# Weight conversion two steps ahead in the first block, an unconditional first single tile, and expert weights requested in halves

## The chip, the cores and the metric

The kernel runs on one core of one Trainium2 chip. Its engines work side by side, each through its own queue in program order: TensorE (PE, matmuls; PEld is its weight load), VectorE (DVE), ScalarE (ACT), GpSimd (POOL) and SyncE (SP, which only issues DMAs here). They wait for each other through semaphores. The metric is the device time of one execution in microseconds.

## The reference

Attention with pooled keys and values, then a dense feed-forward layer, then a layer of routed experts; each stage's output is the next one's input.

```python
k_p = k.reshape(B, H, Sp, pool, D).mean(axis=3)        # B=8, H=8, S=576, D=64, pool=8
v_p = v.reshape(B, H, Sp, pool, D).mean(axis=3)
scores = scale * np.matmul(q, k_p.transpose(0, 1, 3, 2))
attn = softmax(scores)                                 # over 72 pooled keys
x = (attn @ v_p)  -> [4608, 512]
...
h = x @ w_in                                           # w_in float64 [512, 2048]
g = np.where(h >= 1, h, np.where(h <= -1, 0.0, (h + 1) ** 2 / 4.0))
x = g @ w_out                                          # w_out float64 [2048, 512]
...
expert_idx = np.argmax(x @ w_gate, axis=1)             # 8 experts
for e in range(E):                                     # w1[e] [512, 1024], w2[e] [1024, 512]
    h = np.maximum(xe @ w1[e], 0.0)
    out[mask] = gate_w[mask, None] * (h @ w2[e])
```

w_in and w_out arrive as float64. With the inputs that reference.py draws, experts 0, 4, 6 and 7 get 3905, 577, 14 and 112 tokens and the others none, that is 31, 5, 1 and 1 tiles of 128 tokens.

## The kernel before

**Join of attention and feed-forward.** The 36 token tiles are cut into ten blocks (`BLK`: 3, then seven of 4, then 3 and 2). Three tiles (`HEAD`) go through attention first, by a hand-written order (`line`). Then the loop over `steps` runs block j and hidden slice m of 16: `f1(j, m + 2)` computes a slice of 128 hidden units two steps ahead (`AHEAD`), `slot(j, 2m)` does side work, `f2(j, m)` multiplies slice m by its piece of w_out, and `slot(j, 2m + 1)` does side work again. Side work is attention of the next block's tiles (`run_units`: `u_qt` transposes q, `u_sc_all` makes scores and their exponential, `u_turn_p`, `u_place_p` and `u_pv` the rest), pooling of k and v (`kv`), and, in block 0 only, `tick`.

**tick.** In block 0 the float64 weights are fetched and turned into two float32 parts, high and low, held in W (first layer) and WO (second layer). A tick takes three pieces of w_in or w_out at three stages: ACT converts (`convert_a`, lines 522 and 526), DVE merges bits (`convert_b`, lines 534 and 537, handed out by `mix`), ACT writes the high part (`convert_c`, line 544) and POOL the low part (`low_part`, line 264); SP stores the WO piece to DRAM for the later blocks and requests a raw piece five ticks ahead. The list `order` sets which piece each tick takes. `FG` holds f1's results: lines 595 (DVE), 596 (ACT), 600 (DVE), 601 (ACT) and 264 (DVE). `later` and `flush` hand work of one slot to the next flush.

**Experts.** The expert with most tokens goes first, in groups of 4 tiles (lines 977 to 994); the tiles that are left are "single tiles" (`last_slot`). With the counts above these are seven: five of expert 4, one of 6, one of 7. Before a single tile of a new expert, ACT and DVE turn the staged float32 weights (ST1, ST2) into high and low parts (`cvt1_half`, lines 1060 and 1061; `cvt2`, lines 1052 and 1053), inside a branch on a table entry (`if_changed`). SP requests the next expert's w1 into ST1 and w2 into ST2 (`fetch_next`, line 1086) by DMAs that run or not by another table entry: in the kernel before, at the first tile of an expert. A skipped one appears in the trace as an issue of about 0.07 us. Per single tile PE runs `u_h` (1023 to 1025) into two banks, ACT writes them to EH (1026), PE transposes EH (1031), and `u_y2` (1042 to 1044) gives the output. DMA completions are counted on eight queue lanes taken in turn; after branches of different length join, the write of EH's second half waits for the lane count that the taken branch reaches with its last request.

Of the kernel before, what the change touches and what calls it, by code (L numbers as in the profile page):

```python
# [13 lines left out]
ACTF = mybir.ActivationFunctionType  # L14
# [10 lines left out]
def attention_ffn_routed_experts_kernel(  # L25
# [278 lines left out]
    def u_sc_all(t):  # L304
        pbs = [bank(), bank()]
        for c in range(4):
            for g in range(2):
                toks = slice(64 * g, 64 * g + 64)
                kb = KB[(t * 128 + 64 * g) // S % 2]
                for i in range(2):  # L310
                    rows = slice(64 * i, 64 * i + 64)
                    nc.tensor.matmul(pbs[i][toks, c * SP_:(c + 1) * SP_],  # L312
                                     qt_of(t)[rows, c * 128 + 64 * g:c * 128 + 64 * g + 64],
                                     kb[rows, c], start=True, stop=True)
        sc, sc3, smx = sc_of(t), sc3_of(t), smx3[:, t % 3]
        for i in range(2):
            src = pbs[i][:, 0:4 * SP_].rearrange("p (h c) -> p h c", h=4)
            hs = slice(i, H, 2)
            nc.vector.tensor_reduce(out=smx[:, hs], in_=src, axis=AX.X, op=ALU.max)
            mix()  # L320
            nc.vector.tensor_tensor(out=sc3[:, hs], in0=src,
                                    in1=smx[:, hs].to_broadcast([128, 4, SP_]), op=ALU.subtract)
        nc.scalar.activation(out=sc, in_=sc, func=ACTF.Exp, scale=1.0 / 64)
        wide[0] = True
        finish(t)

    smx3 = sb.tile([128, 3, H, 1], F32, name="smx3")
    ssm3 = sb.tile([128, 3, H, 1], F32, name="ssm3")
# [174 lines left out]
    def load_raw(m, o, i):  # L503
        if o:
            src = w_out[m * 128:(m + 1) * 128, :].bitcast(I32).rearrange("p (a x) -> p a x", a=8)
            nc.sync.dma_start(out=RB[i], in_=src)
        else:
            src = w_in[:, m * 128:(m + 1) * 128].bitcast(I32)
            src = src.rearrange("(c p) (a x) -> p c a x", p=128, a=2)
            for c in range(KD):  # L510
                nc.sync.dma_start(out=RB[i][:, 2 * c:2 * c + 2], in_=src[:, c])

    def cvt_dst(i):
        m, o = order[i]
# [33 lines left out]


    FIRST, MORE = AHEAD + 2, 1  # L550
    order = [(m, 0) for m in range(FIRST)] + [(0, 1)]
    PER = []
    n = FIRST
    for m in range(1, KF):
        more = min(MORE, KF - n)
        order += [(m, 1)] + [(n + i, 0) for i in range(more)]
        PER.append(1 + more)
        n += more
    PER.append(0)
    CAHEAD = order.index((1, 1)) - 1  # L560
    ticks = [0]

    def more_raw(i):
# [307 lines left out]
    def table_2():  # L871

        V = Steps()
        st, en, t1, t2 = tv["st"], tv["en"], tv["t1"], tv["t2"]
        V.tensor_reduce(out=tv["tot"], in_=tv["nte"], axis=AX.X, op=ALU.add)
        V.tensor_tensor(out=tv["tot"], in0=tv["tot"], in1=tv["beg"], op=ALU.subtract)
        V.tensor_copy(TB[:, 3:4], tv["tot"])

        def following(end, nx, hn):

            V.tensor_scalar(t1, st, end, None, op0=ALU.is_equal)
            V.tensor_tensor(out=t1, in0=t1, in1=tv["nte"], op=ALU.mult)
            V.tensor_scalar(t1, t1, 0.0, None, op0=ALU.is_gt)
            V.tensor_reduce(out=tv["hn"], in_=t1, axis=AX.X, op=ALU.add)
            sel(V, "nx", "io")
            V.tensor_copy(nx, tv["nx"])
            if hn is not None:
                V.tensor_copy(hn, tv["hn"])

        following(tv["ntf"], TB[:, 6:7], TB[:, 7:8])  # L890
        V.tensor_tensor(out=t1, in0=tv["ind"], in1=en, op=ALU.mult)
        V.tensor_reduce(out=tv["enj"], in_=t1, axis=AX.X, op=ALU.add)
        following(tv["enj"], TB[:, 2:3], None)
        V.tensor_tensor(out=t1, in0=tv["ind"], in1=tv["io"], op=ALU.mult)
        V.tensor_reduce(out=tv["ej"], in_=t1, axis=AX.X, op=ALU.add)
        V.tensor_scalar(tv["jp"], tv["js"], -1.0, None, op0=ALU.add)
        V.tensor_scalar(t1, st, tv["jp"], None, op0=ALU.is_le)
        V.tensor_scalar(t2, en, tv["jp"], None, op0=ALU.is_gt)
        V.tensor_tensor(out=t1, in0=t1, in1=t2, op=ALU.mult)
        sel(V, "ep", "io")  # L900
        V.tensor_tensor(out=tv["ch"], in0=tv["ej"], in1=tv["ep"], op=ALU.not_equal)
        V.tensor_tensor(out=tv["jp"], in0=pcol, in1=tv["tot"], op=ALU.is_lt)
        V.tensor_tensor(out=tv["ch"], in0=tv["ch"], in1=tv["jp"], op=ALU.mult)
        V.tensor_copy(TB[:, 0:1], tv["ch"])
        V.tensor_tensor(out=tv["ch"], in0=tv["ch"], in1=tv["hn"], op=ALU.mult)
        V.tensor_copy(TB[:, 1:2], tv["ch"])
        return V.ops
# [161 lines left out]
        for i in range(2):  # L1069
            cvt2(hf, i)  # L1070

    def if_changed(j, f, engines):
        r = nc.values_load(TB[j:j + 1, 0:1], engines=engines, min_val=0, max_val=1)
        with tc.If(r > 0):
            f()

    def fetch_next(j, which, hf=None, col=(1, 2)):

        cv = nc.values_load(TB[j:j + 1, col[0]:col[0] + 1], engines=[SP], min_val=0, max_val=1)
        ev = nc.values_load(TB[j:j + 1, col[1]:col[1] + 1], engines=[SP], min_val=0, max_val=NE - 1)  # L1080
        src, dst = ((w1, ST1), (w2, ST2))[which]
        src = src[bass.ds(ev, 1)].rearrange("o (c p) f -> p (o c) f", p=128)
        if hf is not None:
            cs = slice(4 * hf, 4 * hf + 4)
            src, dst = src[:, cs], dst[:, cs]
        nc.sync.dma_start(out=dst, in_=src, cond=cv > 0, cond_hint=False)


    with tc.manual_schedule():
# [6 lines left out]
        def head_pool(i, eng):  # L1096
            pool_kv(0, i, raw0[i], eng)
# [26 lines left out]
        hu[1][0]()  # L1124
        for c in range(2, 4):
            u_kt_pair(0, c)
        hu[0][2]()
        for i in (8, 10, 12):
            head_pool(i, nc.gpsimd)
        hu[1][2]()  # L1130
        head_pool(9, nc.vector)
        tick()
        hu[2][0]()
        flush()
        head_pool(14, nc.gpsimd)
        head_pool(11, nc.vector)
        hu[2][2]()
        head_pool(13, nc.vector)
        head_pool(15, nc.vector)
        load_pair(0)  # L1140
        load_pair(1)
        tick()
        flush()
        kv = deque([pair_step(c) for c in range(4)] + [kv_step(1, i) for i in range(H, 2 * H)])
        line = [(0, 3), (0, 5), (1, 3), (0, 6), (1, 5), (2, 3), (1, 6), (2, 5), (2, 6)]
        for i, (t, n) in enumerate(line):
            hu[t][n]()
            flush()
            if i in (1, 4, 6):
                tick()  # L1150
        while ticks[0] < CAHEAD + 3:
            tick()
        banks.clear()
        banks.extend(ps[6:8])
# [16 lines left out]
        def slot(j, s):  # L1171

            want = min(state["units"], -(-(s + 1) * state["units"] // (22 if j == NB - 2 else 29 - 2 * AHEAD + 2)))
            wide[0] = False
            run_units(want - state["done"])
            state["done"] = max(want, state["done"])
            flush()
            if j == 0:
                for _ in range(min(1, PER[s // 2]) if s % 2 == 0 else PER[s // 2] - 1):
                    tick()  # L1180
                if kv:
                    kv.popleft()()
            for _ in range(2 if j >= NB - 2 else 0 if wide[0] else 1 + s % 2):
                if todo:
                    todo.popleft()()
# [27 lines left out]
        for m in range(AHEAD):  # L1213
            f1(0, m)
            flush()
        for g, (j, m) in enumerate(steps):
            if m == 0:
                if j:
# [76 lines left out]
        nq = nc.values_load(TB[0:1, 5:6], min_val=0, max_val=NQ)  # L1295

        def first_weights():
            if_changed(0, cvt1_all, [ACT, DVE])
            fetch_next(0, 0)

        def step_a(qn):
            for m in range(AHEAD):
# [66 lines left out]
        def last_slot(j):  # L1369
            if j + DEEP + 1 < MAXR:  # L1370
                fetch_last(j + DEEP + 1)
            if_changed(j, lambda: cvt2_half(0), [ACT, DVE])
            fetch_next(j, 1, 0)
            if j and j + DEEP < MAXR:
                r_gather(j + DEEP)
            u_h(j, 0)
            u_h(j, 1)
            u_th(j % 2, 0, bank())
            if j + 1 < MAXR:
                if_changed(j + 1, lambda: cvt1_half(0), [ACT, DVE])  # L1380
            if j:
                y_end(j - 1)
            if j and j + DEEP - 1 < MAXR:
                r_tx(j + DEEP - 1)
            u_th(j % 2, 1, bank())
            if j + 1 < MAXR:
                if_changed(j + 1, lambda: cvt1_half(1), [ACT, DVE])
                fetch_next(j + 1, 0)
            if_changed(j, lambda: cvt2_half(1), [ACT, DVE])
            fetch_next(j, 1, 1)  # L1390
            u_y2(j % 2, 0, ps[4 + j % 2])

# [45 lines left out]
```

## Time and profile before

| | |
|---|---|
| time, median of 3 runs | 1418.43 us (1416.07 to 1423.02) |
| the profiled execution's own time | 1422.48 us |
| its span (first to last instruction) | 1420.5 us |
| PE busy | 1363.9 us, 96% of the span |
| DVE, ACT, POOL busy | 769.4, 434.3, 360.0 us |
| mean granted TensorE clock | 0.98 of full speed |

PE is busy almost throughout, so 56.6 us of the span are without a matmul, and the share of the clock below full speed is in the first 160 us and near the end. A row of waits names the waiting engine and line, what released it, the total in us, how often, and the longest. A row of a timeline gives start, duration, engine, line, operation, output and input, count, and in brackets the idle time just before and its releaser.

### The profile page before, as it was taken

The numbers are of one execution on the slowest core, as the hardware profiler recorded it, in microseconds if no ns is written. First come the engines' busy times: TensorE is split into PE (matmuls) and PEld (weight loads), VectorE is DVE, ScalarE is ACT, GpSimd is POOL, SyncE is SP. The second block draws the span as 40 slices with busy tenths as digits, with TensorE's granted clock in tenths as the row PEclk, the third lists the DMA queues.
The fourth block names the chain that finished last, engine by engine and source line by source line (L and its number), as shares of the span: only waits on it lengthen the run. The fifth ranks groups of instructions, "written<-read, shape, count | busy, mean of one in ns | idle before, by whom it ended". The sixth has DMA issues, their size and how long they took to land.

```text
span 1420.5 us, 22119 instructions
## 1 busy us (share of the span) xinstructions
PE 1363.9 (96%) x8082; PEld 1119.8 (79%) x8082; DVE 769.4 (54%) x1573; ACT 434.3 (31%) x729; POOL 360.0 (25%) x517
## 2 busy tenths in 40 slices
PE   5888999999999999999999999999999999999897
PEld 4766778878878878788788788889878888888685
DVE  5677557566666666675666556456433223333335
ACT  4566432222232223223222233342111111112234
POOL 4284644203304202413310011031231121110211
PEclk9889999999999999999999999999999999999999
DMA  8687557446546445644553344572543322332504
GB/s 223 214 264 239 178 145 208 131 136 184 155 133 181 158 134 178 169 158 142 164 155 109 109 138 157 191 248 75 186 127 104 104 87 76 112 104 74 172 31 156
DMA packets 170414, 213.47 MB, mean 150 GB/s; under 512 B 84167, under 2 KB 115175, under 8 KB 170280
## 3 DMA queue, kind: packets, MB, share of 16 engines
q1 hardware_dynamic: 135704, 102.30, 24.8%
q10 hardware_dynamic: 26784, 88.16, 18.6%
q0 software_dynamic: 7792, 21.35, 4.7%
q8 instruction: 69, 1.13, 0.3%
q14 instruction: 65, 0.53, 0.1%
HBM read 188.30 MB, written 47.03 MB: 166 GB/s over the span
## 4 chain that ended last, share of the span: by engine, by line
PE 80%; issue 6%; DVE 4%; DMA 4%; ACT 2%; POOL 1%; SPq 1%; POOLq 0%; ACTq 0%; another core or an unknown queue 0%; DVEq 0%
PE ps L588 9%; PE ps L616 9%; PE ps L590 9%; PE ps L589 9%; PE ps L617 8%; PE ps L618 8%; PE ps L978 4%; PE ps L979 4%; PE ps L977 4%; PE ps L992 3%; PE ps L993 3%; PE ps L994 3%; PE ps L419 3%; PE ps L312 1%; DMA Y<-in_moe_w_out_dram 1%
## 5 line engine op out<-in xcount | busy, mean ns | idle before, releaser
L588 PE MATMUL ps<-XT,W 128*128 128x512 f32 (+2 forms) x640 | 243.7, 381 | 3.5 <-DVE FG L264 2.0
L590 PE MATMUL ps<-XT,W 128*128 128x512 f32 (+2 forms) x640 | 237.9, 372 | 4.6 <-POOL W L264 4.6
L616 PE MATMUL ps<-WO,FG 128*128 128x512 f32 x576 | 233.3, 405 | 5.0 <-ACT WO L544 4.9
L589 PE MATMUL ps<-XT,W 128*128 128x512 f32 (+2 forms) x640 | 238.0, 372 | 0.0
L617 PE MATMUL ps<-WO,FG 128*128 128x512 f32 x576 | 228.5, 397 | 6.5 <-POOL WO L264 6.5
L618 PE MATMUL ps<-WO,FG 128*128 128x512 f32 x576 | 227.3, 395 | 0.0
L596 ACT ACTIVATE FX<-FX,half 128x512 f32<-128x512 f32 (+2 forms) x152 | 104.0, 684 | 388.3 <-DVE FX L595 356.3
L595 DVE TENSOR_SCALAR FX<-ps 128x512 f32<-128x512 f32 (+2 forms) x152 | 96.8, 637 | 120.1 <-PE ps L590 118.2
L588 PEld LDWEIGHTS ps<-XT,W 128*128 128x128 f32 x640 | 122.2, 191 | 27.2 <-DVE FG L264 2.8
L714 POOL DMA_INDIRECT perm_d<-idt,POSI x36 | 35.3, 981 | 416.2 <-DVE SM L700 352.9
L590 PEld LDWEIGHTS ps<-XT,W 128*128 128x128 f32 x640 | 121.7, 190 | 23.4 <-POOL W L264 5.2
L983 DVE SCALAR_TENSOR_TENSOR FG<-ps,FG 128x512 fp32r<-128x512 f32 (+1 forms) x64 | 43.2, 675 | 177.7 <-ACT FG L982 175.2
L600 DVE TENSOR_TENSOR ps<-FX,ps 128x512 f32<-128x512 f32 (+2 forms) x152 | 97.6, 642 | 75.7 <-ACT FX L596 75.7
L589 PEld LDWEIGHTS ps<-XT,W 128*128 128x128 f32 x640 | 122.1, 191 | 17.6
L616 PEld LDWEIGHTS ps<-WO,FG 128*128 128x128 f32 x576 | 109.5, 190 | 31.0 <-ACT WO L544 5.6
L617 PEld LDWEIGHTS ps<-WO,FG 128*128 128x128 f32 x576 | 109.9, 191 | 27.9 <-POOL WO L264 7.8
L618 PEld LDWEIGHTS ps<-WO,FG 128*128 128x128 f32 x576 | 109.9, 191 | 23.8
L601 ACT ACTIVATE FG<-ps 128x512 fp32r<-128x512 f32 (+2 forms) x160 | 88.9, 555 | 120.2 <-DVE ps L600 105.7
L264 DVE TENSOR_TENSOR FG<-ps,FG 128x512 fp32r<-128x512 f32 (+2 forms) x160 | 100.7, 629 | 43.4 <-ACT FG L601 41.3
L252 POOL TENSOR_TENSOR AT<-AT 72x256 f32<-72x256 f32 x106 | 81.1, 765 | 135.2 <-DMA AT<-in_v_dram 67.5
L982 ACT ACTIVATE FG<-ps 128x512 fp32r<-128x512 f32 (+1 forms) x64 | 37.4, 585 | 246.3 <-PE ps L979 232.7
L977 PE MATMUL ps<-XT,W 128*128 128x512 f32 (+1 forms) x256 | 98.9, 386 | 1.4 <-ACT XT L961 1.4
(228 smaller groups left out, 2174.2 us busy)
## 6 DMA issues: line engine op xcount, KB each, us to landing
WO<-wo_d ACTq DMA_DIRECT2D x144, 512.0 KB
AT<-in_moe_w_dram SPq DMA_DIRECT2D x10, 2048.0 KB
AT<-in_moe_w_dram SPq DMA_DIRECT2D x14, 1024.0 KB
p_d<-AT SPq DMA_DIRECT2D x29, 384.0 KB
AT<-in_v_dram SPq DMA_DIRECT2D x59, 144.0 KB
wo_d<-WO SPq DMA_DIRECT2D x16, 512.0 KB
AT<-in_k_dram SPq DMA_DIRECT2D x56, 144.0 KB
PT<-p_d SPq DMA_DIRECT2D x58, 128.0 KB
```

The lines of the kernel that those rows point to most:

```text
L264: eng.tensor_tensor(out=lo, in0=x, in1=r32(hi), op=ALU.subtract)
L588: nc.tensor.matmul(o, wi(m, 0, c), xh, start=(c == 0), stop=False)
L589: nc.tensor.matmul(o, wi(m, 0, c), xl, start=False, stop=False)
L590: nc.tensor.matmul(o, wi(m, 1, c), xh, start=False, stop=(c == KD - 1))
L595: nc.vector.tensor_scalar(r, o, -1.0, 1.0, op0=ALU.max, op1=ALU.min)
L596: nc.scalar.activation(out=r, in_=r, func=ACTF.Square, scale=0.5, bias=half)
L600: nc.vector.tensor_tensor(out=o, in0=r, in1=o, op=ALU.max)
L601: nc.scalar.activation(out=gh, in_=o, func=ACTF.Copy)
L616: nc.tensor.matmul(o, gh, WO[:, g % 4, 0], start=(m == 0), stop=False)
L617: nc.tensor.matmul(o, gh, WO[:, g % 4, 1], start=False, stop=False)
L618: nc.tensor.matmul(o, gl, WO[:, g % 4, 0], start=False, stop=(m == KF - 1))
L977: nc.tensor.matmul(o, e1(0)[:, c, ms], xh, start=(c == 0), stop=False)
```

## The change

- `order` gets (1, 1) right behind (0, 1), so that every piece of w_out from the second on is taken one step earlier than before; `PER` and `CAHEAD` follow. The number of pieces is the same.
- In `slot(0, s)` the tick stands ahead of the units and of flush, not behind them. Two of the early ticks stand behind f1(0, 0) and f1(0, 1).
- In `u_sc_all` of tiles 3 to 8 the exponential is handed to `later`, so it stands behind the flush's other work.
- In the head, the q transpose of tile 2 comes ahead of the first tick, and one v pooling goes from DVE to POOL.
- A raw piece of w_in is requested by one DMA in place of four.
- The first single tile converts its weights without a branch, and the next expert's weights are requested at the last tile of an expert, not at the first; w1 is requested in two halves by columns.

```diff
@@ u_sc_all
-        nc.scalar.activation(out=sc, in_=sc, func=ACTF.Exp, scale=1.0 / 64)
         wide[0] = True
-        finish(t)
+
+        def exps():
+            nc.scalar.activation(out=sc, in_=sc, func=ACTF.Exp, scale=1.0 / 64)
+            finish(t)
+        if HEAD <= t < TURN0:
+            later.append(exps)
+        else:
+            exps()
@@ load_raw
-            src = src.rearrange("(c p) (a x) -> p c a x", p=128, a=2)
-            for c in range(KD):
-                nc.sync.dma_start(out=RB[i][:, 2 * c:2 * c + 2], in_=src[:, c])
+            nc.sync.dma_start(out=RB[i].rearrange("p (c a) x -> p c (a x)", a=2),
+                              in_=src.rearrange("(c p) x -> p c x", p=128))
@@
-    order = [(m, 0) for m in range(FIRST)] + [(0, 1)]
+    order = [(m, 0) for m in range(FIRST)] + [(0, 1), (1, 1)]
...
-    for m in range(1, KF):
+    for m in range(2, KF):
...
-    PER.append(0)
-    CAHEAD = order.index((1, 1)) - 1
+    PER += [0, 0]
+    CAHEAD = order.index((2, 1)) - 1
@@ table_2
-        following(tv["ntf"], TB[:, 6:7], TB[:, 7:8])
+        following(tv["ntf"], TB[:, 6:7])
+        V.tensor_tensor(out=tv["ch"], in0=tv["ntf"], in1=tv["beg"], op=ALU.is_equal)
+        V.tensor_tensor(out=tv["ch"], in0=tv["ch"], in1=tv["hn"], op=ALU.mult)
+        V.tensor_copy(TB[:, 7:8], tv["ch"])
...
+        V.tensor_scalar(tv["ep"], tv["js"], 1.0, None, op0=ALU.add)
+        V.tensor_tensor(out=tv["ch"], in0=tv["enj"], in1=tv["ep"], op=ALU.is_equal)
+        V.tensor_tensor(out=tv["ch"], in0=tv["ch"], in1=tv["jp"], op=ALU.mult)
         V.tensor_tensor(out=tv["ch"], in0=tv["ch"], in1=tv["hn"], op=ALU.mult)
         V.tensor_copy(TB[:, 1:2], tv["ch"])
@@ fetch_next
-        if hf is not None:
+        if hf is not None and which:
             cs = slice(4 * hf, 4 * hf + 4)
             src, dst = src[:, cs], dst[:, cs]
+        elif hf is not None:
+            fs = slice(hf * 512, (hf + 1) * 512)
+            src, dst = src[:, :, fs], dst[:, :, fs]
@@ the head
-        while ticks[0] < CAHEAD + 3:
+        while ticks[0] < CAHEAD + 1:
             tick()
@@ slot
             wide[0] = False
+            if j == 0:
+                for _ in range(min(1, PER[s // 2]) if s % 2 == 0 else PER[s // 2] - 1):
+                    tick()
             run_units(want - state["done"])
             state["done"] = max(want, state["done"])
             flush()
-            if j == 0:
-                for _ in range(min(1, PER[s // 2]) if s % 2 == 0 else PER[s // 2] - 1):
-                    tick()
-                if kv:
-                    kv.popleft()()
+            if j == 0 and kv:
+                kv.popleft()()
@@ the loop's start
         for m in range(AHEAD):
             f1(0, m)
             flush()
+            tick()
@@ first_weights, last_slot
-            if_changed(0, cvt1_all, [ACT, DVE])
-            fetch_next(0, 0)
+            cvt1_all()
+            for hf in range(2):
+                fetch_next(0, 0, hf)
...
-                if_changed(j + 1, lambda: cvt1_half(0), [ACT, DVE])
+                of_tile(j + 1, lambda: cvt1_half(0))
+                fetch_next(j + 1, 0, 0)
...
-                if_changed(j + 1, lambda: cvt1_half(1), [ACT, DVE])
-                fetch_next(j + 1, 0)
+                of_tile(j + 1, lambda: cvt1_half(1))
+                fetch_next(j + 1, 0, 1)
```

What this moves on the engines, at three places. The first is ACT in block 0, where the scores of tile 5 are made; before (L323 is the exponential, L601 f1's result FG, L544 the high part of WO or W):

```order
L596 ACTIVATE AT<-AT,half 128x384
L323 ACTIVATE AT<-AT 128x576
L601 ACTIVATE FG<-ps_73 128x384
L544 ACTIVATE WO<-FX 128x512
L522 ACTIVATE FX<-WG 128x512
L526 ACTIVATE WG<-WG 128x512
L544 ACTIVATE W<-FX 128x512
```

The same place of the change (lines are shifted: L326 is the exponential, L606 FG, L549 the high part):

```order
L601 ACTIVATE AT<-AT,half 128x384
L549 ACTIVATE WO<-FX 128x512
L527 ACTIVATE FX<-Y 128x512
L531 ACTIVATE WG<-Y 128x512
L606 ACTIVATE FG<-ps_73 128x384
L326 ACTIVATE AT<-AT 128x576
L549 ACTIVATE W<-FX 128x512
```

The WO piece went from behind the exponential to ahead of FG, and it is a piece for one step later; the W piece still stands behind the exponential.

The second place is ACT in the head, before (L323 the exponentials of tiles 0 and 1, L522 and L526 the first tick, L362 the copy of tile 2's transposed q, then the exponential of tile 2):

```order
L323 ACTIVATE AT<-AT 128x576 x2
L522 ACTIVATE FX<-Y 128x512
L526 ACTIVATE WG<-Y 128x512
L362 ACTIVATE AT<-ps_75 128x512
L323 ACTIVATE AT<-AT 128x576
```

And in the change:

```order
L326 ACTIVATE AT<-AT 128x576 x2
L368 ACTIVATE AT<-ps_75 128x512
L326 ACTIVATE AT<-AT 128x576
L527 ACTIVATE FX<-Y 128x512
L531 ACTIVATE WG<-Y 128x512
```

The copy of q and the exponential of tile 2 went ahead of the first tick.

The third place is ACT at the first single tile, before (L1060 and L1052 convert w1 and w2, L1026 writes EH; L1073 and L1074 load a table entry and branch on it):

```order
L1074 COMPARE_AND_BRANCH
L1060 ACTIVATE W<-AT 128x2x512 x4
L1074 UNCONDITIONAL_BRANCH x2
L1355 UNCONDITIONAL_BRANCH
L1393 TENSOR_LOAD TB
L1073 TENSOR_LOAD TB
L1073 ISA x2
L1074 COMPARE_AND_BRANCH
L1052 ACTIVATE W<-AT 128x1024 x2
L1074 UNCONDITIONAL_BRANCH x2
L1026 ACTIVATE FX<-ps_72 128x512
L1026 ACTIVATE FX<-ps_73 128x512
```

And in the change (L1070, L1062, L1036 are the same three operations):

```order
L1070 ACTIVATE W<-AT 128x2x512 x4
L1373 UNCONDITIONAL_BRANCH
L1412 TENSOR_LOAD TB
L1062 ACTIVATE W<-AT 128x1024 x2
L1036 ACTIVATE FX<-ps_72 128x512
L1036 ACTIVATE FX<-ps_73 128x512
```

The two branches of the first single tile are gone; the conversions and the writes of EH follow each other in the same order.

## Rows read from the trace of the kernel before

**Rows 1.** The page: granted clock in 40 slices of 35.5 us, in tenths.

```profile
PEclk9889999999999999999999999999999999999999
```

**Rows 2.** Waits of PE in the first 250 us: total, times, longest.

```profile
PE ps L617 <- POOL WO L264: 6.5, 3, 2.8
PE ps L312 <- ACT AT L362: 6.2, 1, 6.2
...
PE ps L616 <- ACT WO L544: 4.9, 3, 2.0
PE ps L590 <- POOL W L264: 4.6, 2, 2.6
...
PE ps L588 <- DVE FG L264: 1.7, 1, 1.7
```

**Rows 3.** Busy time of each engine in block 0 from its second step on.

```profile
core 0: us, PE busy (x) PEld busy (x) DVE busy (x) ACT busy (x) POOL busy (x), PEclk, DMA share, GB/s
57.80:155.84 98.04, 81.76 (x568) 68.42 (x566) 73.30 (x132) 64.46 (x116) 61.02 (x68) 0.85 0.71 229
```

**Rows 4.** The timeline around one of block 0's stalls.

```profile
94.66 0.68 ACT L323 ACTIVATE AT<-AT 128x576 f32<-128x576 f32 x1 [3.22 <-DVE AT L321]
...
95.62 0.62 ACT L544 ACTIVATE WO<-FX 128x512 fp32r<-128x512 f32 x1
...
96.29 0.50 PE L616 MATMUL ps<-WO,FG 128*128 128x512 f32 x1 [1.38 <-ACT WO L544]
...
97.82 1.72 POOL L264 TENSOR_TENSOR WO<-FX,WO 128x512 fp32r<-128x512 f32 x1
...
99.60 0.79 PE L617 MATMUL ps<-WO,FG 128*128 128x512 f32 x1 [2.81 <-POOL WO L264]
```

**Rows 5.** Windows of 1 us around that stall; columns as in group 3.

```profile
97.00:98.00 1.00, 0.00 (x0) 0.00 (x0) 0.51 (x1) 1.00 (x3) 1.00 (x2) 0.77 0.96 298
...
104.00:105.00 1.00, 1.00 (x7) 1.00 (x6) 0.81 (x2) 0.85 (x2) 0.92 (x3) 0.82 0.85 211
```

**Rows 6.** DVE groups by line and form, 57 to 156 us: count, busy, mean ns.

```profile
L537 DVE SCALAR_TENSOR_TENSOR FX<-FX,ps 128x512 int32<-128x512 int32 x25 | 17.1, 683 | 0.9
...
L534 DVE SCALAR_TENSOR_TENSOR ps<-Y,WG 128x512 int32<-128x512 int32 x9 | 8.9, 984 | 0.9 <-ACT WG L526 0.9
```

**Rows 7.** The timeline of the head, at ACT's first tick and at f1's start.

```profile
20.86 0.67 ACT L522 ACTIVATE FX<-Y 128x512 f32<-128x512 f32 x1 [2.10 <-DMA Y<-in_moe_w_in_dram]
...
22.68 1.24 PE L312 MATMUL ps<-AT 64*64 64x72 f32 x32 [6.21 <-ACT AT L362]
...
26.35 0.68 ACT L323 ACTIVATE AT<-AT 128x576 f32<-128x576 f32 x1 [3.72 <-DVE AT L321]
...
39.78 0.69 PE L588 MATMUL ps<-XT,W 128*128 128x384 f32 x1 [1.42 <-DVE XT L426]
```

**Rows 8.** The chain that ended last, at the first single tile.

```profile
1316.13 10.60 DMA AT<-in_moe_w_dram
1326.99 0.61 ACT FX L1026
```

**Rows 9.** Windows of the first single tile; columns as in group 3.

```profile
1321.50:1328.40 6.90, 1.38 (x9) 1.12 (x8) 0.57 (x2) 1.09 (x2) 0.99 (x2) 0.85 0.62 215
1328.40:1333.40 5.00, 5.00 (x14) 3.97 (x13) 2.58 (x4) 2.60 (x3) 1.19 (x1) 0.52 0.49 189
```

**Rows 10.** Waits of PE from 1000 us on.

```profile
PE ps L1031 <- ACT FX L1026: 5.5, 1, 5.5
PE ps L1024 <- DVE W L1061: 1.8, 2, 1.2
...
PE ps L1042 <- ACT W L1052: 1.2, 1, 1.2
```

**Rows 11.** SP and ACT timeline where the last expert's w1 is requested and used.

```profile
1384.88 2.28 SPq L1086 DMA_DIRECT2D AT<-in_moe_w_dram  x2
...
1393.54 2.01 ACT L1060 ACTIVATE W<-AT 128x1024 fp32r<-128x1024 f32 x2 [4.19 <-DMA AT<-in_moe_w_dram]
```

## The prediction on record

> **What bounds the kernel now.** I read the clock first [rows 1]: TensorE is granted full speed nearly everywhere, and what is missing lies in the first four slices, in the head and block 0. Outside them PE is busy, so a gain can come only from places where PE waits or runs slow. The list of PE's waits names those in block 0 [rows 2]: the second-layer weights, 4.9 us for their high part (ACT) and 6.5 us for their low part (POOL), and the first-layer weights, 4.6 us for the low part; in the head, 6.2 us for the copy of tile 2's q. The window over block 0 from its second step on [rows 3] gives the size: 98.04 us, PE busy for 81.76, so 16.28 us of waits, of which the three weight rows are 16.0. The mean granted clock there is 0.85. [...]
>
> The timeline shows how one of those stalls comes about [rows 4]. ACT's exponential of the scores waits 3.22 us for DVE, and the high part of WO stands behind it at 95.62; PE's line 616 waits for that, the low part follows at 97.82 to 99.54 on POOL, and line 617 waits 2.81 us more. TensorE is still at full clock when it stops, falls to the low level during the stall, and is back only near 104.2 [rows 5]. A late conversion is paid twice: in the wait and in the slow stretch behind it.
>
> Near the end, the chain that ended last goes through a 10.60 us transfer from 1316.13 to ACT's second write of EH at 1326.99 [rows 8]. The transfer is the request for expert 6's w1, which no one needs for four more tiles; the write waits for the queue lane that it sits on. PE waits 5.5 us there [rows 10].
>
> **Term 1, block 0.** Each WO piece is now taken a whole step earlier and ahead of the slot's units, and the exponential stands behind it. In the stall of [rows 4] PE needed the piece 1.38 us before its high part and 4.4 us before its low part was there; a step is 98.04 / 14 = 7.0 us with stalls and about 5 without, so it comes in time. The WO rows are 11.4 of 16.0 us of waits [rows 2], 71%. With the same share of the slow clock (8.7 us) they are worth 20.1 us. The exponential does not vanish: the W piece still stands behind it. In the example W's high part would follow the exponential's end (95.3) by 0.6 us and its low part by 1.3 to 1.7 more, so it is ready at about 97.5, and PE, not held up by WO, would need it at about 97.3 (nine matmuls of the second layer at 0.23 us each and a unit behind 94.3). I take 1 us off for it: 19 us.
>
> Bounds: the ceiling is the next engine. DVE is busy for 73.30 us of the window [rows 3], so the gain can't pass 98.04 - 73.30 = 24.7 us. The floor is that W's waits grow as WO's go: I set 5 us.
>
> [...] On DVE, line 537 reads one operand from PSUM and takes 683 ns; line 534, which reads both from SBUF, takes 984 ns on average in one form [rows 6], while POOL is busy 62% of the window [rows 3]. [...]
>
> **Term 2, the head.** ACT was idle 2.10 us before 20.86 for raw weights that its first tick needs, and tile 2's q was copied only behind that tick; PE waited until 22.68 [rows 7]. The copy is now ahead of the tick, so it can start at 20.86 - 2.10 = 18.76, take 0.6 and let PE start at about 19.4: 3.3 us earlier. One tick more (1.2 us of ACT) then stands behind tile 2's exponential, so about 2.1 reach f1's start, now 39.78 [rows 7]. The first f2 needs only the first WO piece, which has the time of two f1 calls. DVE is relieved of one pooling, POOL takes it while it waits for sums. I take 2.5 us; bounds 0 and the whole wait, 6.2.
>
> **Term 3, the first single tile.** Expert 4 has five tiles, so at its first tile the request is now skipped, and nothing large sits on the lane. Of the 6.90 - 1.38 = 5.52 us without a matmul [rows 9] about 0.5 stay, because the second transposes still need ACT's 0.6 us write. The next 5.00 us had a mean clock of 0.52 with PE busy throughout: 2.4 us lost, of which I take 2. Together 7.0 us. The two branches gone save ACT and DVE time that PE doesn't wait for once the request is away: nothing. Bounds 0 (a skipped request that holds its lane) and 7.9.
>
> **Term 4, the last tiles.** Requests move from an expert's first tile to its last. Expert 6 is asked for at tile 4 and not at tile 0, so both of the last changes of expert happen as one did before: w1 asked for at 1384.88, used at 1393.54 after ACT had waited 4.19 us [rows 11], PE waiting 1.8 us for w1 and 1.2 for w2 [rows 10]. Asking in halves lets the first half go as soon as its half of the stage is converted, about 4 us earlier. I take the two as equal: 0. Bounds: 3.0 us won, or 3.0 lost at the change to expert 6.
>
> **Edits at nothing.** One request for a w_in piece in place of four saves SP's issue time. PE's waits name the conversions, not raw data [rows 2]; without that cover a late piece would show as ACT waiting for a DMA, at 2.1 us each as in the head. The few added small DVE operations that fill the table lie beside matmuls, under the last dense block, where PE's clock and work are full [rows 1].
>
> **Sum.** 19 + 2.5 + 7 + 0 = 28.5 us. Against the profiled execution (1422.48 us; span 1420.5 and 2 around it) that gives 1394.0; that execution was 4.05 above the median of the runs, 1418.43, from which it gives 1389.9. I predict **1390 us**.
>
> **Rivals.**
> - A, the forecast: waits for WO go, W's stay small. 1377 to 1400. For it: the cause in [rows 4] is a place in a queue, and the place changes. Chance 0.58.
> - B, block 0 becomes bound by DVE and by W behind the exponential, and gives 5 to 14 us, not 19. For it: DVE's 73.30 us and [rows 6]; the W rows of [rows 2] exist already. Against it: 25% of DVE's time is free. With 8 us the time is 1418.4 - 8 - 2.5 - 6 = 1402. Chance 0.25.
> - C, the stalls only change their name: each WO wait becomes a W or DMA wait of the same length, with its slow stretch, and only the first single tile's 7 us come: 1411.4, at the edge of what can be told from no change. For it: DMA share 0.71 in the window [rows 3]. Against it: no row of [rows 2] waits for raw weights. Chance 0.10.
> - D, slower. The tick's three ACT operations (0.62 [rows 4], 0.67 [rows 7] and the like, 1.9 us) now stand between f1's square and the copy to FG, and so before PE gets f1's bank back. [...] Against it: PE waited for FG once before, 1.7 us [rows 2], and the bank is needed only two f1 later. Chance 0.05.
>
> What is left, 0.02, is none of these. A measurement of this kernel can tell about 0.5%, 7 us, from no change. A and B are faster by more than that (0.83), C and part of the rest the same (0.12), D slower (0.05). The range must reach over B: from the ceilings of the terms (24.7 + 6.2 + 7.9 + 3.0 = 41.8, 1377) to B's slow end, 1376 to 1410; A's own is 1377 to 1400.
>
> **What would show it.** Right: in the changed profile PE's waits for WO in block 0 are below 2 us, the block from its second step on takes about 79 us with a mean clock over 0.95, f1 starts near 37.5, the first single tile has less than 1 us between its transposes, and one more short wait for w1 or w2 stands two tiles before the end. B would show as PE waits for W or FG with DVE over 85% busy in the block; C as equal idle time under another name; D as a wait at nearly every f1. The prediction is wrong if PE's waits in block 0 stay above 10 us, if the second write of EH still waits for a DMA, or if the two last changes of expert cost more than 6 us.

## The result and the profile after

| | before | after |
|---|---|---|
| time, median | 1419.03 us (1416.07 to 1423.02, 4 runs) | 1403.26 us (1401.01 to 1404.88, 4 runs) |
| ratio to before | | 0.9895, 95% interval 0.9876 to 0.9914 |
| the profiled execution's own time, span | 1422.48, 1420.5 us | 1404.79, 1402.8 us |
| PE busy | 1363.9 us | 1357.5 us |

The change saves 15.8 us of the 28.5 forecast: 13 us short of 1390, inside the range (1376 to 1410), and at the time of rival B (1402). Of the terms, the first is far off; the comparison of the two profiles, stage by stage, in us:

| | predicted | the two profiles |
|---|---|---|
| block 0 from its second step on | 19 | 98.04 - 90.68 = 7.4 |
| head, start of f1 | 2.5 | 39.78 - 38.11 = 1.7 |
| first single tile, from its first matmul to the next tile's input transposes | 7.0 | 26.15 - 18.73 = 7.4 |
| the last two single tiles, from the input transposes of the last but one to the end of the span | 0 | 29.28 - 25.79 = 3.5 |

Between block 0 and the first single tile the change is 2.3 us longer, mostly in short waits of PE, none over 2.5 us; with that the sum is the 17.7 us between the spans.

The granted clock by slices, of the page after (answering to [rows 1]): every slice is now at nine tenths or more.

```profile
PEclk9999999999999999999999999999999999999999
```

PE's waits in the first 250 us after (answering to [rows 2]; total, times, longest), and block 0 as one window (answering to [rows 3], the same columns):

```profile
PE ps L425 <- DMA PT<-p_d: 6.2, 3, 3.5
...
PE ps L312 <- ACT AT L368: 2.8, 1, 2.8
PE ps L595 <- POOL W L264: 2.7, 4, 0.8
PE ps L593 <- DVE FG L264: 2.6, 2, 2.1
PE ps L593 <- ACT W L549: 1.9, 2, 1.2
PE ps L366 <- DVE AT L321: 1.6, 2, 1.1
```

```profile
56.05:146.73 90.68, 76.46 (x567) 62.88 (x565) 77.64 (x127) 60.76 (x110) 55.63 (x61) 0.93 0.76 245
```

No wait for WO is left: 11.4 us of waits are gone, as forecast. In their place PE waits 6.2 us for PT, the transposed attention weights P that go to DRAM (`p_d`) and come back; W's rows are 2.7 + 1.9 = 4.6 us, what they were. PE is idle for 90.68 - 76.46 = 14.2 us of the block, 2.1 less than before, and busy for 5.3 us less, at a clock of 0.93 against 0.85: together the 7.4 us. DVE is busy for 77.64 of 90.68 us, 86%.

The first single tile and the last change of expert after, as windows (answering to [rows 9]; the first in one piece), and PE's waits there (answering to [rows 10]):

```profile
1309.19:1327.92 18.73, 18.43 (x84) 14.69 (x85) 7.29 (x8) 5.97 (x9) 4.42 (x4) 1.00 0.15 54
...
1377.01:1389.66 12.65, 12.50 (x62) 10.15 (x61) 11.03 (x13) 8.85 (x12) 2.67 (x2) 1.00 0.74 248
```

```profile
PE ps L1053 <- DVE W L1063: 0.7, 1, 0.7
...
PE ps L1041 <- ACT FX L1036: 0.3, 1, 0.3
```

### The profile page after: what moved, and what is told of

Read it like the earlier page. It is cut to its first block, busy times and chain, and to the rows that moved or that the text cites. A ratio compares the mean times of both kernels' runs of the same rounds, so it can differ in the third digit from the quotient of the medians.

```text
span 1402.8 us, 22101 instructions
## 1 busy us (share of the span) xinstructions
PE 1357.5 (97%) x8082; PEld 1112.8 (79%) x8082; DVE 778.1 (55%) x1577; ACT 433.7 (31%) x729; POOL 358.7 (26%) x520
## 5 line engine op out<-in xcount | busy, mean ns | idle before, releaser
L601 ACT ACTIVATE FX<-FX,half 128x512 f32<-128x512 f32 (+2 forms) x152 | 104.0, 684 | 386.0 <-DVE FX L600 348.2
L621 PEld LDWEIGHTS ps<-WO,FG 128*128 128x128 f32 x576 | 108.5, 188 | 26.4 <-issue 3.0
L623 PEld LDWEIGHTS ps<-WO,FG 128*128 128x128 f32 x576 | 108.6, 188 | 23.7
L606 ACT ACTIVATE FG<-ps 128x512 fp32r<-128x512 f32 (+2 forms) x160 | 88.8, 555 | 123.9 <-DVE ps L605 112.2
L622 PEld LDWEIGHTS ps<-WO,FG 128*128 128x128 f32 x576 | 108.7, 189 | 19.8
```

What stands on the lines that cost most here:

```text
L601: nc.scalar.activation(out=r, in_=r, func=ACTF.Square, scale=0.5, bias=half)
L606: nc.scalar.activation(out=gh, in_=o, func=ACTF.Copy)
L621: nc.tensor.matmul(o, gh, WO[:, g % 4, 0], start=(m == 0), stop=False)
L622: nc.tensor.matmul(o, gh, WO[:, g % 4, 1], start=False, stop=False)
L623: nc.tensor.matmul(o, gl, WO[:, g % 4, 0], start=False, stop=(m == KF - 1))
```

## The experiments

All twelve ran beside the kernel before, whose median was 1417.60 us beside e1 to e4, 1416.31 beside e5 to e8, 1419.33 beside e9 and e10 and 1416.13 beside e11 and e12. So kernels are compared by their ratios, not by their times. "Block 0" is its length from the second step on; the waits in it are PE's, by what they wait for; both come from one profile of each kernel. Times are in us.

| | time | ratio to before, interval | block 0 | WO | W | PT | others |
|---|---|---|---|---|---|---|---|
| before | 1419.03 | | 98.04 | 11.4 | 4.6 | 0.3 | 0 |
| the change | 1403.26 | 0.9895 (0.9876 to 0.9914) | 90.68 | 0 | 4.6 | 6.2 | 3.2 |
| e1, no single tiles | 1410.33 | 0.9944 (0.9923 to 0.9964) | 88.43 | 0 | 3.2 | 7.2 | 3.1 |
| e2, single tiles alone | 1408.22 | 0.9942 (0.9919 to 0.9964) | 94.31 | 12.0 | 4.6 | 0 | 0 |
| e3, exponential inline | 1406.64 | 0.9922 (0.9901 to 0.9944) | 93.57 | 0 | 7.0 | 2.0 | 8.9 |
| e4, no addition | 1399.75 | 0.9876 (0.9852 to 0.9899) | 87.60 | 0 | 4.2 | 5.5 | 4.1 |
| e5, P x V later | 1401.30 | 0.9888 (0.9873 to 0.9904) | 89.26 | 0 | 0.2 | 2.3 | 8.9 |
| e6, tick behind | 1409.00 | 0.9941 (0.9927 to 0.9955) | 97.61 | 0 | 13.2 | 1.5 | 0 |
| e7, old order | 1402.17 | 0.9893 (0.9878 to 0.9908) | 88.86 | 0 | 3.1 | 7.6 | 3.3 |
| e8, W ahead | 1401.68 | 0.9890 (0.9875 to 0.9906) | 94.83 | 0 | 0 | 9.7 | 6.1 |
| e9, P turned early | 1403.12 | 0.9885 (0.9862 to 0.9907) | 88.57 | 0 | 1.7 | 8.9 | 3.1 |
| e10, both e9 and e4 | 1400.48 | 0.9870 (0.9850 to 0.9890) | 88.68 | 0 | 1.6 | 8.8 | 0.6 |
| e11, e9 with raw behind | 1401.56 | 0.9891 (0.9871 to 0.9910) | 89.13 | 0 | 6.4 | 5.4 | 2.2 |
| e12, three loads of PT left out | 1400.82 | 0.9888 (0.9864 to 0.9913) | 89.55 | 0 | 6.0 | 1.2 | 4.1 |

**Which part gave what (e1, e2).** e1 takes the parts on table, branches and requests back to the kernel before; e2 is the kernel before with these parts alone.

```diff
-            cvt1_all()
-            for hf in range(2):
-                fetch_next(0, 0, hf)
+            if_changed(0, cvt1_all, [ACT, DVE])
+            fetch_next(0, 0)
...
```

> The change without its part on the single tiles (branches, request and its halves as before). By the comparison of the two profiles, the first single tile gave 7.4 us and the tail 3.5 us. If both are the doing of that part, this kernel loses them: 1403.3 + 10.9 = 1414.2 us, ratio to before 0.9966. If the tail's 3.5 us are only the difference of two executions: 1410.7, ratio 0.994.

> The kernel before with the change's part on the single tiles alone. If the first single tile's 7.4 us and the tail's 3.5 us are its doing: 1419.0 - 10.9 = 1408.1 us, ratio 0.992; if only the 7.4: 1411.6, ratio 0.995. The block 0 waits for WO must stand as before (11.4 us).

By ratio, head and block 0 give 0.56% (7.9 us) and the single tiles 0.58% (8.2 us); their sum, 1.14%, is the change's 1.05% within the intervals. e1 came out at its second value (0.994); the first, 0.9966, lies outside its interval. e2 lies between its two ratios, and its interval holds both. By the profiles the last two tiles gain all the same, 28.9 us in e1 and 26.3 in e2. What is smaller there is the gain at the first single tile: e1 waits 3.5 us at it, not 5.5 as in [rows 10], and takes 23.13 us, not 26.15, where e2 takes 18.68. So the single tiles are worth 4.5 + 2.6 = 7.1 us by this pair of profiles and 7.4 + 3.5 = 10.9 by the first pair. e2's block 0 has the instructions of before and takes 94.31 us, not 98.04:

```profile
57.27:151.58 94.31, 77.70 (x569) 64.33 (x566) 72.42 (x131) 63.54 (x114) 59.54 (x66) 0.91 0.72 237
```

So one execution's block 0 differs from another's by up to 3.7 us; over two profiles of each kind (before and e2, the change and e1) it went from 96.2 to 89.6, by 6.6 us.

**Which edit in block 0 did it (e7, e6, e3).** e7 puts the order of pieces back, e6 the tick behind the units and flush, e3 the exponential inline.

```diff
-    order = [(m, 0) for m in range(FIRST)] + [(0, 1), (1, 1)]
+    order = [(m, 0) for m in range(FIRST)] + [(0, 1)]
```

> The change with the old order of pieces (WO not one step earlier, one piece less in the head); the tick stays ahead of the units and the exponential in flush. If the step earlier for WO is what took its waits away: they come back, 3 to 8 us of them, 1408 to 1414. If the tick ahead of the units and of the exponential is enough: no WO wait over 1 us, and f1 starts 1 us earlier: 1401 to 1404.

```diff
-            if j == 0:
-                for _ in range(min(1, PER[s // 2]) if s % 2 == 0 else PER[s // 2] - 1):
-                    tick()
             run_units(want - state["done"])
             state["done"] = max(want, state["done"])
             flush()
+            if j == 0:
+                for _ in range(min(1, PER[s // 2]) if s % 2 == 0 else PER[s // 2] - 1):
+                    tick()
```

> The change with the tick behind the units and flush, as before the change; the order of pieces, one step earlier for WO, stays, and the exponential stays in flush. WO is asked for one step earlier, so by the sum on record its waits stay away even so; the tick's conversions no longer stand ahead of FG, P's store and PT's load. If the tick's place does not matter: 1402 to 1405. If the WO pieces need both: WO waits of 2 to 6 us come back, 1406 to 1412. If the tick ahead of the units holds up P's way on SP: PT waits shrink, 1398 to 1401.

```diff
-        if HEAD <= t < TURN0:
-            later.append(exps)
-        else:
-            exps()
+        exps()
```

> The change with the exponential of tiles 3 to 8 back in its old place, ahead of FG. The WO piece stays ahead of it, so the WO waits stay away by every theory. If W behind the exponential is the bound, the exponential only trades places with FG's copy and both W and FG wait for DVE's scores: FG comes up to 3 us later at four tiles, PE waits for FG, 1405 to 1410 us. If the way of P through DRAM is the bound, P starts 0.5 to 1 us sooner at each tile, three waits shrink: 1400 to 1402. If DVE is the bound, the order on ACT changes little: 1402 to 1405.

With the tick ahead of the units the step earlier for WO adds nothing: without it (e7) no WO wait comes back. The place of the tick is worth 0.46% (6.5 us), and the intervals of e6 and of the change do not touch. The place of the exponential is worth 0.27% (3.8 us) by the medians, but the intervals overlap, so its price is likely and not shown. PE's waits in block 0 of e6:

```profile
PE ps L595 <- POOL W L264: 9.5, 5, 3.3
PE ps L593 <- ACT W L549: 3.7, 2, 2.2
PE ps L425 <- DMA PT<-p_d: 1.5, 1, 1.5
```

There WO comes a step early and is never waited for. But as WO's 11.4 us go, W's waits grow from 4.6 to 13.2, which none of e6's three cases had, and block 0 is as long as before. In time e6 (0.9941) is where e2 is (0.9942), which has none of the edits in the head and block 0. That is rival C's mechanism, and it is the tick ahead of the units that takes it away. In e3 the waits move to W's low part and to FG, the two that stand behind the exponential then:

```profile
PE ps L592 <- POOL W L264: 7.0, 4, 3.5
PE ps L590 <- DVE FG L264: 5.3, 4, 1.9
```

**What bounds block 0 now: one wait? (e5, e9, e11, e12).** The new wait is for PT. The third product of P and v in block 0, with the issue of its load of PT, before and in the change:

```profile
123.08 1.60 SPq L399 DMA_DIRECT2D PT<-p_d  x3
129.35 1.09 PE L419 MATMUL ps<-PT,VS 72*64 72x128 f32 x16
```

```profile
121.28 1.17 SPq L405 DMA_DIRECT2D PT<-p_d  x3
125.19 1.98 PE L425 MATMUL ps<-PT,VS 72*64 72x128 f32 x16 [3.48 <-DMA PT<-p_d]
```

PE came to this product at 129.35 us before and at 125.19 - 3.48 = 121.71 in the change, 7.6 us earlier; the load was issued only 1.8 us earlier. At the two products before it PE came 2.0 and 3.2 us earlier, the loads 0.6 and 1.9. e5 moves its user one unit later, e9 its maker one unit earlier, e11 puts the raw request behind the units besides, and e12 leaves out the loads of three tiles.

```diff
+        def late(t):
+            return turned(t) and t < HEAD + blocks[1][1] - 1
...
+                order = [(t, 1)] + [(t - 2, 6)] * late(t - 2)
+                order += [(t - 1, 3), (t, 2), (t - 1, 5), (t + 1, 0), (t - 1, 4)]
+                order += [(t - 1, 6)] * (not late(t - 1))
```

> The change with the P x V product of tiles 3, 4 and 5 one unit later (behind the f2 that it stood ahead of), so that the way of P through DRAM has one step more. If P's way is a bound of block 0 by itself: the three waits for PT (6.2 us in the profile, with a slow stretch of 6 us behind the longest) go and nothing takes their place: -5 to -8 us against the change, 1395 to 1398, ratio to before 0.984 to 0.986. If DVE is the bound and the wait for PT only the place where PE shows it: W and FG waits grow by as much, 1401 to 1404, ratio 0.989 to 0.99.

```diff
-                order = ((t, 1), (t - 1, 3), (t, 2), (t - 1, 5), (t + 1, 0), (t - 1, 4), (t - 1, 6))
+                order = ((t - 1, 3), (t, 1), (t, 2), (t - 1, 5), (t + 1, 0), (t - 1, 4), (t - 1, 6))
```

> The change with DVE's two transposes of P, and P's store behind them, one unit earlier in the order (ahead of the empty unit that stands before them). In the changed profile P of a tile is normalised at 101.1 us and transposed only at 112.95, its load is released at 121.28 and PE waits until 125.19; one unit is about 3 us. Nothing else moves, and no bank is held longer. If P's way through DRAM is a bound of block 0: the three waits for PT (6.2 us) shrink to under 1.5, 1396 to 1399, ratio to before 0.985 to 0.987. If DVE is the bound and PT only the place where PE shows it: W, FG and scores' waits grow by as much, 1400 to 1403, ratio 0.988 to 0.99.

```diff
-            more_raw(n - 1 + NRB)
+            (held.append if hold[0] else more_raw)(n - 1 + NRB)
...
             run_units(want - state["done"])
+            while held:
+                more_raw(held.pop(0))
```

> The kernel with the transposes of P one unit earlier, and besides the raw piece that a tick requests (512 KB) goes on SP behind the slot's units, so behind P's store and PT's load, not ahead of them. With the transposes early, SP hardly waited for P's store (0.8 us), but PT's loads still took 4.7 to 7.9 us from their issue to PE, with a raw piece issued just ahead of them, and PE still waited 8.9 us. If the load's place behind the raw piece in the queue is what makes it late: each PT wait shrinks by 1.3 us and more, the three to under 5 us, block 0 to 84 to 86 us, 1397 to 1400. If the transfers share one limit whatever their order: PT waits stay at 6 to 9 us, or ACT waits for raw pieces, 1401 to 1404.

```diff
     def u_place_p(t):
+        if HEAD < t < HEAD + blocks[1][1]:
+            return
```

> The change without the loads of PT for tiles 4, 5 and 6, whose P x V then uses the P of tile 3: three tiles of the output get another P. Of the three waits for PT in block 0 the second and the third (4.9 us in the profile, with the slow stretch behind the longest) have nothing to wait for. If P's way is a bound by itself: block 0 from its second step on falls by 5 to 8 us, to 82 to 85 us. If PE only waits there in place of waiting for the conversions: W, FG and scores' waits grow, block 0 stays at 87 to 91 us.

Each came out at the case without a gain: the ratio of each lies inside the change's interval. e5 is spoilt as a test: the PT waits fall to 2.3 us, but the product now holds its bank until just before the next scores, and PE waits for that:

```profile
PE ps L312 <- DVE XT L432: 8.0, 3, 3.2
PE ps L425 <- DMA PT<-p_d: 2.3, 2, 1.4
```

In e9 the store is early enough (SP's wait for it, in the list of SP's waits, falls from the first row, of the change, to the second, of e9), yet PE waits for PT longer (8.9 us, 6.2 in the change), because the load itself takes longer: 5.6 to 7.9 us from its issue to PE's product at the three waits, 3.9 to 4.9 in the change. e11, with the raw piece behind, takes 3.5 us off e9's waits, and W's waits rise by 4.7.

```profile
SPq L405 <- DMA p_d<-AT: 7.8, 3, 5.1
```

```profile
SPq L405 <- DMA p_d<-AT: 0.8, 1, 0.8
```

e12 is the clear case. The second and third wait have nothing to wait for, and block 0 is 89.55 us. Two windows of the change, at the longest PT wait and behind it, and two of e12 at the same place (columns as in [rows 3]):

```profile
122.00:125.00 3.00, 0.00 (x0) 0.00 (x0) 2.97 (x6) 3.00 (x7) 1.72 (x2) 0.83 0.78 202
125.00:128.00 3.00, 2.81 (x18) 2.42 (x19) 1.61 (x3) 3.00 (x6) 1.71 (x2) 0.50 0.68 246
```

```profile
120.00:123.00 3.00, 3.00 (x18) 2.56 (x19) 2.90 (x4) 2.97 (x6) 2.09 (x2) 0.58 0.24 61
123.00:126.00 3.00, 3.00 (x15) 2.29 (x12) 2.73 (x6) 3.00 (x7) 1.29 (x1) 0.50 0.78 310
```

Block 0 of e12 as one window:

```profile
55.44:144.99 89.55, 78.24 (x569) 63.93 (x566) 77.66 (x127) 60.82 (x110) 55.71 (x61) 0.92 0.73 238
```

While PE stands for PT, DVE is busy for 2.97 of 3.00 us and ACT for all of them, with conversions among the rest. Without the wait PE goes on at once, and the slow stretch comes all the same, behind shorter waits for scores (0.97 us) and W (0.76 and 0.75). PE is idle for 11.3 us of e12's block, 2.9 less than in the change, but busy for 1.8 more at a lower clock. The other profiles pair the same way: e5 has 11.4 us idle at a clock of 0.91 and e10 11.2 at 0.90, against 13.8 at 0.96 in e4 and 13.9 at 0.95 in e11, and these blocks are all 87.6 to 89.6 us long. So PE either waits or runs slow, and comes out at nearly the same time.

Which engine ACT waits for is in its list of waits in the change's block 0:

```profile
ACT FG L606 <- DVE ps L605: 13.8, 10, 4.2
ACT AT L601 <- DVE AT L600: 8.4, 6, 3.6
ACT FX L601 <- DVE FX L600: 4.9, 4, 2.5
ACT AT L326 <- DVE AT L321: 4.1, 2, 2.7
```

ACT waits 31.2 us, always for DVE. It waited 35.0 us for DVE in the longer block before, so this was not brought by the change. By its own list DVE waits 10.9 us, 4.5 of them for ACT and 6.4 for PE. Neither waits for a DMA, so raw weights are not late there.

**DVE and GpSimd (e4, e10), and W by itself (e8).** e4 drops the addition of 1e-9 to the softmax sums, e10 does so with e9's order, e8 converts one W piece more in the head.

```diff
-            nc.vector.tensor_scalar(ssm, ssm, 1e-9, None, op0=ALU.add)
```

> The change without the addition of 1e-9 to the softmax sums of the tiles from 3 on and of the head's three; a sum is 1 or more, so in float32 the value stays the same. In the changed block 0 this 128x8 addition takes 1164 ns on DVE (170 before the change) and ends when GpSimd's operation ends. If DVE, held up by GpSimd, is the bound of block 0: 5 x 1.1 us of DVE gone, -3 to -5 us, 1398 to 1400. If DVE only stands in the order and P's way through DRAM is the bound: P is 1 us earlier at four tiles, its three waits shrink by up to 3 us, 1400 to 1402, and the W waits stay. If neither: 1403.

> The transposes of P one unit earlier and no addition of 1e-9 (the value is the same in float32). If both are bounds of their own: the sum of the two, about -3 and -5 us, 1394 to 1396. If both act on the same way of P: no more than the better of the two alone, 1397 to 1400.

```diff
-    FIRST, MORE = AHEAD + 2, 1
+    FIRST, MORE = AHEAD + 3, 1
```

> The change with one more w_in piece converted in the head, so that every W piece of block 0 comes a step earlier; one tick more (1.2 us of ACT) in the head. If W behind the exponential and scores is a bound by itself: its 4.6 us of waits go and the block gets 3 to 6 us shorter, less 0.5 to 1.2 us in the head: 1398 to 1401. If DVE is the bound: W waits go and others grow, 1402 to 1405.

e10 and e4 have the lowest ratios, 0.9870 and 0.9876, and e10 adds nothing clear to e4. By time e4 came out at its first case, e10 and e8 just beside their second. The intervals of both overlap the change's, so a gain over the change is likely but not shown. DVE's busy time in the block falls by 6.3 us (77.64 to 71.36), the block by 3.1 against the change's profile and 0.8 against e1's. In e8 W's waits are gone; PT's (9.7 us, 6.2 in the change) and FG's (1.2, 0.5) grow. Its profile is that of the slowest of its five executions (1406.16 us, median 1401.68), so its block of 94.83 us is not to be set against the others.

## Why the prediction was right and wrong

- **The number and the account.** The change is faster, as forecast, by 15.8 us where 28.5 were forecast. It lies in the range because the range was drawn to reach over rival B; it lies outside the forecast's own 1377 to 1400. Two of the forecast's signs for block 0 failed (90.68 us, not about 79; a clock of 0.93, not over 0.95), and one of its signs of being wrong came true: PE's waits in block 0 stay at 14.2 us, above 10. So the account of block 0 was wrong in size. That term 4, priced at nothing, made up for 2.6 to 3.5 us of it is luck.
- **Term 1, the mechanism.** Right that the WO waits are a place in a queue and go with it: 11.4 us to 0. The step earlier, on which the sum rested, does bring WO in time by itself (e6). But that alone gives no time, because W's waits grow to 13.2 us; and with the tick ahead of the units it is not needed (e7). The time comes from the tick's place (e6).
- **Term 1, the size.** The step that failed is "they are worth 20.1 us", with 1 us off for W. It priced the removed waits as if PE's other waits stayed where they were. The 8.7 us of slow clock in the 20.1 are the author's estimate and no run shows them; they come to 71% of the 0.15 of full speed that is missing over 81.76 us of busy PE [rows 3]. In the stall of [rows 4] the clock was 1.00 from 96 to 97 us and 0.50 from 98 to 104. In [rows 2] the block had next to no wait but WO and W; PE came late enough that P's way through DRAM was covered (0.3 us of waits for PT). In the change PE comes to the third product 7.6 us earlier and P's load only 1.8, and 6.2 us of waits for PT appear. PE's idle time in the block fell by 2.1 us, not by 11.4, and the clock gave 5.3 us, not 8.7. The prediction had named DMA waits as rival C's, and set them aside because no row of before shows one for raw weights: P's transfer was not looked at.
- **The profile of before.** Its block 0 of 98.04 us was a long one (94.31 in e2), so the 7.4 us of the pair of profiles is likely too much; the two pairs give 6.6.
- **Rivals.** The time is B's, and half of B's sign is there: DVE is 86% busy, and ACT waits 31.2 us for it (35.0 before), but W's waits are 4.6 us as before and FG's 0.5. PE's largest wait is for a DMA, C's kind; with its last two waits left out (e12) the block stays as long. So B holds as an outcome; that DVE is its cause is possible and not shown. D is out: FG waits within block 0 are 0.5 us.
- **DVE beside GpSimd.** The prediction set line 534's 984 ns beside line 537's 683 [rows 6], with POOL busy for 62% of the window; the 984 were those of the dearest of line 534's three forms, and its mean was 883 ns. Measured by the groups of DVE by line and form: line 539 (534 before) went from 21.2 us for 24 (883 ns) to 23.3 for 22 (1059 ns), 3.9 us; and the addition of 1e-9, 170 ns five times before, pays 5.0 us more, which nobody had counted. The sum is 8.9 us. What made the two dearer no run shows.

```profile
L539 DVE SCALAR_TENSOR_TENSOR ps<-WG 128x512 int32<-128x512 int32 x11 | 11.6, 1055 | 0.3
L539 DVE SCALAR_TENSOR_TENSOR ps<-Y,WG 128x512 int32<-128x512 int32 x8 | 8.9, 1110 | 0.0
...
L378 DVE TENSOR_SCALAR ssm<-ssm 128x8 f32<-128x8 f32 x5 | 5.8, 1164 | 0.2
L539 DVE SCALAR_TENSOR_TENSOR ps<-AT,WG 128x512 int32<-128x512 int32 x3 | 2.8, 934 | 0.0
```

- **Term 2.** PE goes on at 19.15 us with tile 2's scores (19.4 on record, 22.68 before), but 1.7 us reach f1, not 2.5: between there and f1 PE is idle for 0.8 us more than before and busy for 1.0 more.
- **Term 3.** Right in mechanism and size: before, ACT's write of EH waited 7.3 us for the transfer of expert 6's w1, after for no DMA; PE's wait is 0.3 us, the clock 1.00, 18.7 us for the tile. Over executions the old wait varies (5.5, and 3.5 in e1), so the term is 4.5 to 7.4 us by the two pairs of profiles.
- **Term 4.** 2.6 to 3.5 us won, not 0: the extra change of expert costs nothing (12.27 us between the transposes of those tiles, 12.28 before), and ACT's wait of 4.19 us for w1 [rows 11] is gone altogether. That it is the halves which did this, and not the request's place, was not tried by itself. In the change, where the last expert's second half of w1 is converted, ACT waits 0.37 us and not for a DMA:

```profile
1379.11 2.01 ACT L1070 ACTIVATE W<-AT 128x1024 fp32r<-128x1024 f32 x2 [0.37 <-ACT XT L1044]
```

- **Left open.** What sets block 0 at 88 to 91 us. Taking away two waits for PT (e12), W's waits (e8) or 6.3 us of DVE (e4) each left it at 87.6 or more. That DVE, with ACT behind it, delivers PE's inputs at this rate fits ACT's waits above, but is argued, not shown. The rival is the clock: shorter waits could have been worth their length, had PE not run slow for longer. No run holds the clock fixed, so the two cannot be told apart.

## What to carry to other kernels

In this case the list of waits showed only the last of several late things: PT's waits in block 0 were 0.3 us before and 6.2 in the change, and W's grew from 4.6 to 13.2 in e6, as WO's went. Before the length of a wait is taken as the gain, move PE's next uses forward by that length and look for transfers and conversions that were ready by less, above all round trips through DRAM such as P's, whose 0.3 us told nothing of the 6.2. Where several producers are busy while PE stands (DVE for 2.97 and ACT for 3.00 of the 3.00 us at the longest wait for PT), price the removed wait by what these producers have left to do. Do not take the slow clock's share in proportion to the waits: with the change PE's idle time fell by 2.1 us and its busy time by 5.3, and in e12 another 2.9 us of idle time went and 1.8 us of busy time came back.

## What the hardware showed beyond that

A small DVE instruction took nearly as long here as a large one on GpSimd: 1.08 us for the addition of 1e-9 (128 x 8 elements), 1.28 us for GpSimd's low part of a W piece (128 x 512). The timeline of the change:

```profile
118.37 1.28 POOL L264 TENSOR_TENSOR W<-FX,W 128x512 fp32r<-128x512 f32 x1 [4.34 <-ACT W L549]
...
118.59 1.08 DVE L378 TENSOR_SCALAR ssm<-ssm 128x8 f32<-128x8 f32 x1
```

And before, where the addition took 0.17 us and GpSimd was idle beside it:

```profile
119.24 0.17 DVE L372 TENSOR_SCALAR ssm<-ssm 128x8 f32<-128x8 f32 x1
...
119.79 1.15 POOL L376 TENSOR_TENSOR AT<-AT,ssm 128x576 f32<-128x576 f32 x1 [5.70 <-DMA WG<-in_moe_w_in_dram]
```

In the change GpSimd's instruction ends at 119.65 and the addition at 119.67; all five additions of block 0 end within 0.03 us of one of GpSimd's. What ties the two ends together, no run here shows. With the new order an instruction that it doesn't touch took 1164 ns on average and not 170; its duration in the profile of before was no price for it.
